# The MoE 1 planner's rate for DMA transposes, 290 to 173 bytes per ns, in a kernel of attention and two MoE layers

## The chip, the cores and the metric

The kernel runs on one core of a Trainium2 chip. The metric is the device time of one execution in microseconds (us); lower is better. Times of before are given as the median of three runs; the profile is one further execution.

## What is computed

Attention over 4 batches, 8 heads, 576 tokens and 64 columns a head, with a mask by blocks of 64; its output, 2304 tokens of 512 columns, goes through MoE 1 (one dense layer with an ELU-like function) and MoE 2 (a skip test, a choice of one of 8 experts for each token, and that expert's two matrices). Cut to the operations:

```python
def _attn_ref(q, k, v):                      # 4 x 8 x 576 x 64
    scores = scale * np.matmul(q, k.transpose(0, 1, 3, 2))
    scores = np.where(block_i >= block_j, scores, -1000000000.0)
    attn = softmax(scores)
    return np.matmul(attn, v)

def _moe_ref(x, w_in, w_out):                # 2304 x 512, 512 x 2048, 2048 x 512
    h = x @ w_in
    g = np.where(h > 0.0, h, np.exp(np.minimum(h, 0.0)) - 1.0)
    return g @ w_out

def _moe2_ref(x, w_skip, w_gate, w1, w2):    # 8 experts, 512 x 1024 and 1024 x 512
    do_compute = x @ w_skip > 0
    e_idx = np.argmax(xc @ w_gate, axis=1)   # xc: the rows of x with do_compute
    h = np.maximum(xc[mask] @ w1[e], 0.0)    # for each expert e
    y[mask] = gate_w[mask, None] * (h @ w2[e])
    out[do_compute] = xc + y
```

## The kernel before

The program has two parts. Its first, which takes some 620 us, holds attention, MoE 1, the routing of all tokens and the preparation of the first experts' weights; a planner puts all of it in one order. Its second runs the experts in blocks of 128 tokens, with a small plan for each block.

*Attention* goes by batch b, head pair p and block row i. `s_unit` computes scores into a PSUM tile s (a ring of 3), `x_unit` takes the row maximum on VectorE (mx) and the exp on ACT (e32), `h_unit` and `l_unit` write the normalised weights as two fp16 halves, high and low, into ehl (ACT writes one, VectorE the other). SP then transposes ehl to et with a DMA transpose, and `pv` multiplies et with v (vt) into the PSUM tile xps (one buffer). k and q are split into halves and transposed by DMA in the same manner (kt, qt).

*MoE 1* takes chunks c of 256 tokens, nine of them. `l1` is the first matrix (PSUM h, a ring of 2), `l1a` and `l1b` the function on ACT and VectorE (g), `l2` the second matrix (PSUM y). The first two chunks run in fp32 on the tiles twi and two, the others in fp16 halves (win, wout). The weights come as 64-bit floats: `raw_load` loads 512 KB of words (rw, 16 times w_in and 16 times w_out), `conv` makes fp32 words of them with three VectorE operations. A load waits for the conversion of the fourth load before it.

*Routing*: `post` scales a tile of y, transposes it by DMA (x2t, 256 KB; the very last tile goes through TensorE), `logits` computes nine columns (lp), `route` and `route2` find expert and place on VectorE, with a small matmul (rp), and store them in lists. When the last chunk is routed, the gathers of the first block (gp, from GpSimd) start, each transposed by DMA (mxt). Two blocks of the first experts (`ahead_block`, matmuls ahp and ya) are gathered a chunk earlier and run meanwhile.

*The order.* Every operation of the first part is recorded as a step with its reads and writes (class `Recorder`), and `order` (line 149) plays the steps through: it keeps for each engine the time at which it is free, for each step the time at which its inputs are there, takes the engine that can go on first, and of its ready steps the one recorded first. What comes out is a fixed order of instructions on each engine; on the chip an engine takes them strictly in that order. `_Engine.cost` (line 310) says how long a step takes. For a DMA on SP there are two numbers: how long SP is busy, and for how long the transfer holds the DMA queue. The second moves `dma_free`, the time until which the queue is taken: SP is not given a new transfer more than 3 us before that time, a transfer ends behind it, and what reads its result may be planned 1.0 us after its end.

```python
if e == "sp":
    f = max(f, dma_free - 3.0)
...
    end = max(t + (1.12 if s[1] < 0.6 else 1.3), dma_free) + s[2]
    dma_free = end
```

Of the kernel before, what the change touches and what calls it, by code (L numbers as in the profile page):

```python
# [267 lines left out]
def _count(ap):  # L268
    n = 1
    for _, c in ap:  # L270
        n *= c
    return n
# [15 lines left out]
class _Engine:  # L288
# [21 lines left out]
    def cost(self, op, k):  # L310
        e = self.e
        out = k["out"]
        if e == "sp":
            b = _count(out.ap) * mybir.dt.size(out.dtype)
            if op == "dma_start_transpose":
                return max(1.2, b / 290e3 + 0.35), b / 290e3
            run = min(a.ap[-1][1] * mybir.dt.size(a.dtype) for a in (out, k["in_"]))
            return 0.48, b / 360e3 * (2 if run < 512 else 1)
        n = _count(out.ap[1:])
        sb = all(x.space == bass.MemoryType.SB for x in (out, k.get("in_", out), k.get("in0", out)))  # L320
        if e == "pe":
            if op == "transpose":
                return 0.2, 0.0
            t = n / 2400.0 * (4 if k["lhsT"].dtype == F32 else 1)
            here = out.offset // out.ap[0][0]
            prev, self.rec.last_pe = self.rec.last_pe, here
            return (0.02 if prev == 0 and here == 64 and n < 400 else max(t, 0.01)), 0.0
        if e == "act":
            aps = any(hasattr(k.get(x), "tensor") for x in ("scale", "bias"))
            return (0.094 if sb else 0.051) + n * 0.833e-3 + 0.093 * (aps + ("accum_out" in k)), 0.0  # L330
        if e == "dve":
            if op == "tensor_reduce":
                n = _count(k["in_"].ap[1:])
            aps = any(hasattr(k.get(x), "tensor") for x in ("scalar", "scalar1", "scalar2"))
            x = 1.0
            if op in ("tensor_copy", "tensor_scalar") and sb:
                x = 0.5 if mybir.dt.size(k.get("in_", k.get("in0")).dtype) == 4 else 0.25
            return 0.069 + n * x / 960.0 + 0.061 * aps, 0.0
        if op == "indirect_dma_start":
            return 1.05, 2.0  # L340
        return 0.15, 0.0
# [1471 lines left out]
```

## Time and profile before

| what | us |
|---|---|
| runs, median of three | 803.34 (802.21 to 807.96) |
| the profiled execution | 801.38 |
| its span, from first to last instruction | 799.7 |
| TensorE busy | 699.3 |
| VectorE busy | 585.4 |
| ScalarE (ACT) busy | 526.9 |
| GpSimd (POOL) busy | 98.3 |

The page of the profile gives for each engine the busy time, for 40 equal slices of the span the busy share and the granted TensorE clock, and groups of instructions with the idle time before them and what ended it. Further answers of the trace give sums by stretches of time, the waits between engines, and the instructions in order of time. PE is TensorE, DVE VectorE, ACT ScalarE, POOL GpSimd, and SP issues the DMAs. Most matmuls of the first part are recorded by one helper and so carry one line, L307; they are told apart by their tiles.

### The profile page before, as it was taken

What the parts mean: (1) busy time and instruction counts of PE and PEld (TensorE: products, weight loads), DVE (VectorE), ACT (ScalarE), POOL (GpSimd) and SP (SyncE); (2) the same over time, 40 slices, a digit from 0 to 9 for tenths busy, and PEclk for the clock granted to TensorE, in tenths of its full rate; (3) what the DMA queues carried; (4) which work ended last, traced back from release to release, by engine and by line L of the source; (5) the groups of instructions that cost most, each with busy time, mean ns of one, the idle gap of its engine ahead of it and who ended that gap; (6) DMA issues with size and microseconds to landing.
All of it is one profiled execution on the core that took longest, in us unless ns stands there. A gap on an engine that the chain in (4) does not pass through costs nothing. (4 is left out here: it accounts for less than half of the span.)

```text
span 799.7 us, 18029 instructions
## 1 busy us (share of the span) xinstructions
PE 699.3 (87%) x6586; PEld 461.1 (58%) x6586; DVE 585.4 (73%) x1721; ACT 526.9 (66%) x1166; POOL 98.3 (12%) x185
## 2 busy tenths in 40 slices
PE   0349868999998998999999999999998848998995
PEld 0238524675465655556646667675766635776763
DVE  3866988887998888987789648997876513737810
ACT  4555655999896886886578537673665425868832
POOL 2000000001001100100100100101040432322112
PEclk9999999999999999999999999999999979999998
DMA  9999999976897799898276089271564699989322
GB/s 226 256 204 291 294 299 256 213 130 122 165 176 139 138 181 202 170 197 155 49 125 143 19 162 374 94 225 40 188 181 141 123 236 236 330 240 216 70 29 39
DMA packets 300437, 141.43 MB, mean 177 GB/s; under 512 B 269659, under 2 KB 277989, under 8 KB 299808
## 3 DMA queue, kind: packets, MB, share of 16 engines
q1 hardware_dynamic: 295568, 130.65, 72.7%
q0 software_dynamic: 4752, 9.33, 4.8%
q8 instruction: 60, 0.98, 0.5%
q14 instruction: 57, 0.47, 0.2%
HBM read 76.20 MB, written 13.41 MB: 112 GB/s over the span
## 5 line engine op out<-in xcount | busy, mean ns | idle before, releaser
L307 PE MATMUL h<-xt,win 128*128 128x256 f16 x1344 | 159.5, 274 | 1.4 <-DVE n L307 1.0
L307 PE MATMUL y<-wout,g 128*128 128x512 f16 x672 | 156.5, 380 | 0.0
L307 PEld LDWEIGHTS <-win 128*128 128x128 f16 x1344 | 128.2, 98 | 28.2 <-issue 5.0
L307 PEld LDWEIGHTS <-g 128*128 128x128 f16 x672 | 62.4, 98 | 70.6 <-issue 5.2
L307 ACT ACTIVATE ehl<-e,su 128x64 f16<-128x64 f32 (+4 forms) x208 | 86.2, 470 | 22.7 <-DVE su L307 9.1
L307 ACT ACTIVATE e<-s,mx 128x64 f32<-128x64 f32 (+7 forms) x160 | 78.5, 492 | 34.0 <-DVE mx L307 16.3
L307 DVE SCALAR_TENSOR_TENSOR ehl<-e,su,ehl 128x64 f16<-128x64 f32 (+4 forms) x208 | 85.9, 442 | 9.8 <-ACT ehl L307 9.4
L307 PE MATMUL s<-kt,qt 128*64 128x512 f16 (+7 forms) x640 | 64.7, 306 | 25.6 <-ACT e L307 14.6
L307 DVE TENSOR_REDUCE mx<-s 128x1 f32<-128x64 f32 (+7 forms) x160 | 70.1, 448 | 11.5 <-PE s L307 11.1
L307 PE MATMUL xps<-et,vt 128*64 128x128 f16 (+1 forms) x1440 | 49.7, 220 | 22.0 <-DMA et<-ehl 19.0
L307 POOL MEMSET ehl<- 128x128 f16 x80 | 16.3, 210 | 403.2 <-DMA et<-ehl 284.2
L307 PEld LDWEIGHTS <-vt 128*64 128x64 f16 x1440 | 41.5, 115 | 39.3 <-issue 23.2
L307 PE MATMUL h<-xt,twi 128*128 128x256 f32 x256 | 63.3, 403 | 0.9 <-DVE g L307 0.9
L307 PE MATMUL y<-two,g 128*128 128x512 f32 x128 | 61.7, 613 | 2.4 <-DVE two L307 2.4
L307 PEld LDWEIGHTS <-qt 128*64 128x64 f16 x640 | 28.8, 115 | 57.8 <-issue 40.8
L307 PEld LDWEIGHTS h<-xt,twi 128*128 128x128 f32 x256 | 50.1, 201 | 10.6 <-DVE g L307 1.3
L307 ACT ACTIVATE el<-h,col 128x512 f32<-128x512 f32 x56 | 38.2, 682 | 25.3 <-PE h L307 25.1
L307 PE MATMUL y<-p,hh 128*128 128x512 f16 x192 | 46.0, 393 | 9.5 <-ACT hh L307 9.1
L307 ACT ACTIVATE g<-el,col 128x512 f16<-128x512 f32 x56 | 40.1, 717 | 19.6 <-DVE el L307 19.4
L307 PEld LDWEIGHTS <-hh 128*128 128x128 f16 x288 | 27.7, 99 | 43.1 <-ACT hh L307 9.6
L1450 DVE SCALAR_TENSOR_TENSOR p<-p,n,p 128x1024 f16<-128x1024 f32 x37 | 47.3, 1282 | 5.1 <-ACT p L1449 5.0
L307 PEld LDWEIGHTS <-p 128*128 128x128 f16 x768 | 45.8, 98 | 8.2 <-issue 3.7
(209 smaller groups left out, 1176.1 us busy)
## 6 DMA issues: line engine op xcount, KB each, us to landing
p<-in_moe_w_dram SPq DMA_DIRECT2D x45, 512.0 KB, 6.6
rw<-in_moe_w_in_dram SPq DMA_DIRECT2D x16, 512.0 KB, 5.1
rw<-in_moe_w_out_dram SPq DMA_DIRECT2D x16, 512.0 KB, 7.4
pb<-in_moe_w_dram SPq DMA_DIRECT2D x14, 512.0 KB, 5.6
vflat<-in_v_dram SPq DMA_DIRECT2D x4, 1152.0 KB, 7.3
out_dram<-pay SPq DMA_DIRECT2D x18, 256.0 KB, 3.5
pay_d<-pay SPq DMA_DIRECT2D x18, 256.0 KB, 2.6
raw<-in_k_dram SPq DMA_DIRECT2D x16, 256.0 KB, 3.9
```

Of the source, the lines that this page charges most:

```text
L307: rec.call(e, time, lambda: getattr(self.real, op)(*args, **kw), reads, writes, dma)
L1450: rc.call("dve", 1.2, lambda: nc.vector.scalar_tensor_tensor(out=half(1), in0=raw.t, scalar=sc, in1=half(0), op0=ALU.mult, op1=ALU.subtrac ...
```

## The change

One number in the planner's cost of a DMA transpose: the time for which it holds the queue in the plan is now its bytes at 173 in place of 290 per ns. The time for which SP is busy with it keeps its 290. No operation, tile or buffer changes.

```diff
--- before.py
+++ after.py
@@ -313,7 +313,7 @@
         if e == "sp":
             b = _count(out.ap) * mybir.dt.size(out.dtype)
             if op == "dma_start_transpose":
-                return max(1.2, b / 290e3 + 0.35), b / 290e3
+                return max(1.2, b / 290e3 + 0.35), b / 173e3
             run = min(a.ap[-1][1] * mybir.dt.size(a.dtype) for a in (out, k["in_"]))
             return 0.48, b / 360e3 * (2 if run < 512 else 1)
```

A transpose of 512 KB, the largest, is planned with 3.0 us of the queue in place of 1.8, one of 128 KB, the smallest, with 0.8 in place of 0.5. All engines' orders change, from near the start up to the first blocks of the experts. Three places:

SP's queue while w_out is loaded (rw, in_moe_w_out_dram; et, qt and kt are transposes, vflat a load of 1.2 MB), before:

```order
L307 DMA rw_142<-in_moe_w_out_dram 128x1024
L307 DMA_TRANSPOSE qt_361<-qq_360 128x16x128
L307 DMA vflat_297<-in_v_dram 128x2304
L307 DMA rw_143<-in_moe_w_out_dram 128x1024
L307 DMA rw_144<-in_moe_w_out_dram 128x1024
L307 DMA rw_145<-in_moe_w_out_dram 128x1024
L307 DMA_TRANSPOSE et_336<-ehl_318 128x12x128
```

and after:

```order
L307 DMA rw_142<-in_moe_w_out_dram 128x1024
L307 DMA rw_143<-in_moe_w_out_dram 128x1024
L307 DMA rw_144<-in_moe_w_out_dram 128x1024
L307 DMA vflat_297<-in_v_dram 128x2304
L307 DMA_TRANSPOSE et_336<-ehl_318 128x12x128
L307 DMA rw_145<-in_moe_w_out_dram 128x1024
```

rw_143 and rw_144 moved ahead of the load vflat_297 and of the transpose qt_361, which has seven more w_out loads ahead of it now.

TensorE in batch 1's second half (xps_745 takes et_719 and then et_728; h_746 and h_773 are groups of MoE 1's first matrix, y_720 of its second, s_749 a score of batch 2; each row stands for a run of like ones with their weight loads), before:

```order
L307 MATMUL xps_745<-et_719,vt_384 64x128
...
L307 MATMUL xps_745<-et_719,vt_485 64x128
...
L307 MATMUL xps_745<-et_719,vt_557 64x128
...
L307 MATMUL h_746<-xt_449,win5_589 128x256
...
L307 MATMUL xps_745<-et_728,vt_384 64x64
```

and after:

```order
L307 MATMUL xps_745<-et_719,vt_557 64x128
...
L307 MATMUL h_746<-xt_449,win5_589 128x256
...
L307 MATMUL y_720<-wout3_631,g_724 128x512
...
L307 MATMUL s_749<-kt_667,qt_670 64x64
...
L307 MATMUL h_773<-xt_449,win6_597 128x256
...
L307 MATMUL xps_745<-et_728,vt_384 64x64
```

Behind et_719 stand now, besides the second half of h_746's matmuls, a group of y_720, the score s_749 and half of h_773 before et_728 is used; twelve of h_746's 24 moved ahead of et_719.

TensorE at the hand-over from MoE 1 to the experts (lp_1443 and lp_1445 are the logits of the last chunk's two tiles, rp_1449 its router matmul, ahp and ya the ahead blocks), before:

```order
L307 MATMUL lp_1443<-wgs_78,x2t_1439 128x9
...
L307 MATMUL lp_1445<-wg32_79,x2t_1442 128x9 x4
...
L1078 MATMUL ya_1494<-p20_7394,hha_1488 128x512
...
L307 MATMUL rp_1449<-oh16_1448,tri16_76 128x8
...
L307 MATMUL rp_1449<-oh16_1448,ones16_75 128x8
```

and after:

```order
L307 MATMUL lp_1445<-wg32_79,x2t_1442 128x9 x4
...
L1078 MATMUL ya_1494<-p20_7429,hha_1488 128x512
...
L307 MATMUL lp_1443<-wgs_78,x2t_1439 128x9
...
L307 MATMUL rp_1449<-oh16_1448,tri16_76 128x8
...
L307 MATMUL rp_1449<-oh16_1448,ones16_75 128x8
```

lp_1443 moved behind lp_1445, behind twelve matmuls of ahp and six of ya.

## Rows read from the trace of the kernel before

**Rows 1.** The page: span, busy time of each engine, granted clock in 40 slices.

```profile
span 799.7 us, 18029 instructions
...
PE 699.3 (87%) x6586; PEld 461.1 (58%) x6586; DVE 585.4 (73%) x1721; ACT 526.9 (66%) x1166; POOL 98.3 (12%) x185
...
PEclk9999999999999999999999999999999979999998
```

**Rows 2.** Sums by stage: stretch, length, busy us of each engine, clock, DMA share, GB/s.

```profile
0.00:55.00 55.00, 13.48 (x151) 9.32 (x151) 35.83 (x110) 29.48 (x81) 4.83 (x41) 1.00 1.08 227
55.00:95.00 40.00, 36.96 (x170) 28.66 (x169) 30.51 (x64) 25.99 (x46) 0.32 (x2) 1.00 1.09 289
95.00:150.00 55.00, 44.78 (x349) 21.47 (x347) 48.48 (x142) 33.55 (x73) 1.53 (x8) 0.99 1.10 261
150.00:480.00 330.00, 316.95 (x3197) 201.34 (x3193) 274.79 (x905) 251.13 (x646) 26.54 (x74) 0.99 0.78 145
480.00:605.00 125.00, 124.02 (x944) 83.83 (x941) 104.13 (x275) 78.36 (x112) 15.34 (x21) 1.00 0.57 188
605.00:629.00 24.00, 18.55 (x276) 14.22 (x274) 13.70 (x77) 10.54 (x27) 4.94 (x5) 1.00 0.45 108
629.00:800.00 171.00, 144.52 (x1525) 102.31 (x1521) 77.99 (x153) 97.82 (x185) 44.82 (x35) 0.95 0.71 169
...
150.00:200.00 50.00, 50.00 (x401) 35.30 (x396) 40.90 (x149) 47.18 (x125) 5.53 (x14) 0.97 0.75 148
```

**Rows 3.** Waits, 95 to 150, and TensorE's of 0 to 150: total us, times, longest.

```profile
PE y L307 <- DVE two L307: 2.4, 4, 1.1
...
DVE two L307 <- DMA rw<-in_moe_w_out_dram: 5.7, 5, 2.4
...
PE s L307 <- ACT e L307: 12.1, 9, 2.9
```

**Rows 4.** Waits of TensorE, 150 to 480.

```profile
PE xps L307 <- DMA et<-ehl: 8.3, 9, 1.8
...
PE xps L307 <- DVE qq L307: 1.1, 1, 1.1
```

**Rows 5.** Sums of two stretches: transposes alone, then copies.

```profile
396.00:413.00 17.00, 16.83 (x149) 8.73 (x148) 12.13 (x40) 11.00 (x32) 1.02 (x5) 1.00 0.54 101
483.00:503.00 20.00, 20.00 (x158) 13.89 (x156) 18.01 (x62) 15.01 (x24) 1.23 (x1) 1.00 1.03 372
```

**Rows 6.** TensorE in order of time: start us, us, what, idle before it.

```profile
253.80 2.79 PE L307 MATMUL h<-xt,win 128*128 128x256 f16 x24
...
258.39 0.66 PE L307 MATMUL xps<-et,vt 128*64 128x64 f16 x30 [1.79 <-DMA et<-ehl]
```

**Rows 7.** The same around 295: twelve y, twelve h and the row behind.

```profile
292.77 2.76 PE L307 MATMUL y<-wout,g 128*128 128x512 f16 x12
295.37 1.47 PE L307 MATMUL h<-xt,win 128*128 128x256 f16 x12
296.68 0.45 PE L307 MATMUL lp<-wgs,x2t 128*128 128x9 f16 x12
```

**Rows 8.** The hand-over on TensorE, VectorE, GpSimd and TensorE again.

```profile
609.20 0.46 PE L307 MATMUL lp<-wgs,x2t 128*128 128x9 f16 x12
609.51 1.04 PE L307 MATMUL lp<-wg,x2t 128*128 128x9 f32 x8
610.40 0.83 PE L1078 MATMUL ahp<-mxt,p 128*128 128x128 f16 x12
611.07 1.46 PE L1078 MATMUL ya<-p,hha 128*128 128x512 f16 x6
...
610.46 0.29 DVE L307 COPY lg<-lp 128x9 f32<-128x9 f32 x2
...
619.94 1.12 POOL L307 DMA_INDIRECT gp<-pay_d,lists  x1 [10.04 <-DVE hha L307]
...
628.62 1.50 PE L307 MATMUL hp<-mxt,p 128*128 128x128 f16 x24 [2.72 <-DMA mxt<-gp]
```

## The prediction

> **What bounds the kernel now.** I read the page's head first [rows 1]: the span is 799.7 us, and TensorE is busy for 699.3 of it (87%), more than any other engine, at a granted clock of 0.9 or more in all slices but one. The change adds and removes no instruction, so those 699.3 us stay. What a new order can move is the rest, some 100 us in which TensorE stands idle, and the next question is where it lies. The sums by stage [rows 2] answer it: length less PE busy gives 41.5 us of idle time in 0 to 55, 3.0 in 55 to 95, 10.2 in 95 to 150, 13.1 in 150 to 480, 1.0 in 480 to 605, 5.5 in 605 to 629 and 26.5 behind that.
>
> These stages have different limits. Up to 150 us the DMA share is above 1: the transfers set the pace, TensorE waits. From 150 to 605 TensorE itself is the limit (441 of 455 us). From 605 to 629 the last tokens are routed and gathered. Behind 629 the instructions of each block stand in the same order before and after, so that I leave its 26.5 us as they are.
>
> Of each stage I then read who waits for whom. From 95 to 150 TensorE lost 2.4 us to VectorE's conversion of the w_out words, and VectorE 5.7 us to the loads of these words [rows 3]. From 150 to 480 it lost 8.3 us in nine waits of an xps matmul for the transpose that fills et [rows 4]; with the smaller rows of that answer this is nearly the whole 13.1.
>
> **Which rate is true.** The planner charges a copy 360 bytes per ns and charged a transpose 290. Two stretches of the queue show each kind alone [rows 5]: from 396 us on SP issues only transposes, from 483 us on almost only 512 KB copies. The transposes move 101 GB/s at a DMA share of 0.54, which is 187 for a full share; the copies 372 at 1.03, which is 361. So 360 was right for copies, 290 too fast for transposes by half, and 173 is 8% on the slow side. The new plan thinks of a transpose's landing about as the chip does; it was too hopeful before, and placed consumers so tightly that nine of them waited.
>
> A rule of the Trainium skill speaks against this: "Advanced Engine Details and Errata", section X-Bar Transpose (TRN2), says that transpose DMAs are as fast as regular ones, at 350 to 400 GB/s. By that rule even 290 was too slow and the change makes the plan worse. The trace does not agree for these shapes, 187 against 361, so this gets a small chance only (last rival).
>
> **The change, term by term.** The sum is made on the profiled execution, 801.4 us (its span and 1.7 us around it). The median of the runs shown is 803.3, which is 2.0 more; I stay on the profiled execution's footing.
>
> 0 to 55: no term. The last transpose before the first MoE 1 matmul (et_263) is the 36th transfer of the queue in both orders, with the same 11.9 MB issued ahead of it, and the DMA share there is 1.08. What goes earlier inside this stretch makes something else later by as much.
>
> 55 to 150, the w_out loads: all of them but the third, and the fourth, which stays where it was, come with fewer bytes ahead of them in SP's queue, mostly by 0.5 to 1.7 MB; the first piece of order above shows two of them jumping ahead of a vflat load of 1.2 MB and a qt transpose of 0.5 MB. At the 261 GB/s of 95 to 150 that is 2 to 6 us earlier. The raw loads and transposes that fall behind them are for batch 1, whose scores come only at the end of this stretch. What a load can give back is the wait for it: 2.4 us on TensorE at least as it stands, 5.7 if VectorE, busy for 48.5 of these 55 us, turns every gap of its own into earlier words; nothing if ACT, whose exps and squares the matmuls of this stretch wait for too, is late by itself. I take the row nearest to the end of the chain, TensorE's: **-2.4** (0 to -5.7).
>
> 150 to 480, the xps matmuls: how long a transpose is covered is the matmul work that stands between the last score of its unit and its first use. The second piece of order shows the longest of the nine waits, 1.79 us at 258.39 [rows 6]. New in front of xps_745<-et_728 are six y matmuls and twelve h ones, some four score matmuls aside. Twelve y matmuls took 2.60 us and the twelve h ones behind them 1.31, by the starts of the following rows [rows 7], so the new work is 1.30 + 1.31 = 2.6 us, more than the wait. I went through the other eight in the same way: for six of the nine the order puts 0.9 to 4 us more in front, for three nothing that counts. Six at the mean of 8.3/9 = 0.92 are 5.5 us saved. The work comes from somewhere: three places have less in front than before, et_998 (2.6 us less), xps_1019 (its one PSUM buffer is now asked for straight behind xps_981, with 0.3 us of work between in place of 5.7), and s_411, with 0.2 us behind the score that frees its buffer in place of 5. At 0.92 each they cost 2.8. Sum: **-2.7** (from -9.4, where all the waits for et with the 1.1 beside them go, to +2.8, where the waits only move and the new ones come on top).
>
> 480 to 605: 1.0 us of idle time is there to win or lose; the pieces only change places by one or two. No term.
>
> 605 to 629, the hand-over: this one is a loss that the order shows. Before, the two logits groups of the last chunk (lp_1443, lp_1445) stood together at 609.20 and 609.51 [rows 8], VectorE copied both at 610.46, and the chain went on through routing, list, gather (619.94) and transpose to the first hp matmul at 628.62, with TensorE idle 2.72 us in front of it. After, the plan expects x2t_1439 later and puts lp_1443 behind lp_1445, twelve ahp and six ya matmuls (third piece of order): from 609.20 on 0.89 for lp_1445 and 0.67 for the ahp ones by the starts of the rows, 1.30 for the ya ones as for six y in rows 7, and its own 0.46, together 3.3 us, so it ends at 612.5 in place of about 609.7, and both logits are there 2.0 us later than 610.5. The router's rp matmul also stands three ya matmuls further back (0.65 us), which the delay hides. Behind the late lp stand only the ahead blocks, which fill TensorE meanwhile but run out before 628. The scatter of the first ahead block now stands in front of the first gathers on POOL; that engine was idle for 10.04 us there and ya ends earlier in the new order, so I cost it at nothing; if its o2 is late, it costs its own issue, some 1.1 us as the gather's row has it. Of the 2.0 us I take **+1.7** (0 if the lists' other inputs came last anyway, +3.1 with the scatter).
>
> Sum: 801.4 - 2.4 - 2.7 + 1.7 = **798.0 us**.
>
> **Rivals.**
> *All the waits go* (the plan is now true, everything lands in time): -5.7 - 9.4 and 0 to +1.7 at the hand-over, with 0.85 taken: 787.1 us. For it speaks that the waits for et are short, 1.8 us at most [rows 4], so that a little more cover cures them; against it that ACT and DVE are behind most of these chains.
> *The waits only move*: -2.4, +1.7 and the et waits as long as before: 800.7 us. For it: TensorE is at 96% from 150 to 480, so whatever is put in front of one consumer is missing in front of another.
> *ACT and VectorE become late* (slower): from 150 to 200 ACT is busy 47.2 of 50 us [rows 2]. The new order moves scores, logits and routing of chunk 0 closer together there, so that more VectorE work stands between a score and its et; where this grows more than the cover, the score buffers stay full and TensorE waits for ACT's exp as it does in the first 150 us, 12.1 us in nine waits [rows 3], 1.34 each. From five such waits on it eats the forecast's gain; eight of them are +10.7, with -2.4 and +1.7: 811.4 us.
> *Transposes are as fast as copies*, so that the plan is now further off: no gain from loads or cover, +2.8 for the new places, +1.7: 805.9 us. The two rates of [rows 5] speak against it. It is what the rule of the Trainium skill named above would bring.
>
> **How the numbers follow.** Forecast 0.42 (its own range 793 to 803), all the waits go 0.26, the waits only move 0.15, ACT and VectorE late 0.12, fast transposes 0.05. One per cent, about what a measurement of this kernel tells from no change, is 8 us: below 793.4 lies the first rival with 0.07 of the forecast's tail, 0.33; above 809.4 the slower rival and 0.03 of tails, 0.15; 0.52 between. The range runs from 784, a little past the fast rival's time, to 810, at the near edge of the slow one's, and leaves out about 0.1 at either end.
>
> **What would show it.** Right: in the changed profile TensorE's waits for VectorE's two shrink below 1 us from 95 to 150, the nine xps waits fall to about six in all with half the time, the second logits group of the last chunk ends near 612 and the first hp matmul behind the gathers has more idle time in front than 2.72 us; PE idle from 150 to 480 is near 10 us. Wrong: that idle time stays at 13 or grows with ACT's exp as releaser (third rival), or falls below 5 (first); or et_263 lands earlier or later than before, which would mean that the start is not held by bytes.

## The result and the profile after

| | before | after |
|---|---|---|
| median of four runs | 802.78 us (800.12 to 807.96) | 812.71 us (809.77 to 814.26) |
| ratio, 95% interval | | 1.0103 [1.0064, 1.0143] |
| profiled execution, its span | 801.38, 799.7 us | 809.77, 808.0 us |

The change cost 1.0%. The forecast of 798.0 had the wrong sign, and its range ended 2.7 us short of the median. The profiled execution is the fastest of the four after, so the trace shows 2.9 us less of the loss than the median. The page's head after, which answers to [rows 1]:

```profile
span 808.0 us, 17999 instructions
...
PE 703.2 (87%) x6586; PEld 465.7 (58%) x6586; DVE 589.1 (73%) x1721; ACT 527.5 (65%) x1166; POOL 97.9 (12%) x185
...
PEclk9999998799999999999999999999999889999998
```

TensorE has the same 6586 matmuls and is busy 3.9 us longer. The clock row has a new dip in the seventh and eighth slice (121 to 162 us). Sums by stage of the kernel after (columns as in [rows 2]):

```profile
95.00:130.00 35.00, 29.81 (x176) 13.47 (x176) 33.27 (x76) 18.49 (x38) 0.61 (x3) 1.00 1.08 307
130.00:160.00 30.00, 21.10 (x202) 12.80 (x202) 24.63 (x100) 23.14 (x54) 1.23 (x6) 0.77 0.96 204
160.00:480.00 320.00, 312.42 (x3157) 198.22 (x3157) 269.66 (x876) 247.73 (x631) 26.18 (x73) 0.99 0.81 145
480.00:520.00 40.00, 36.46 (x270) 23.90 (x269) 32.66 (x83) 26.30 (x40) 1.94 (x2) 1.00 0.60 218
...
605.00:640.00 35.00, 25.27 (x343) 20.15 (x342) 15.92 (x86) 14.24 (x34) 7.55 (x8) 0.92 0.61 130
```

and the same stretches of the kernel before:

```profile
130.00:160.00 30.00, 25.93 (x255) 16.63 (x251) 25.89 (x103) 23.46 (x54) 1.23 (x6) 0.94 1.06 222
160.00:480.00 320.00, 306.95 (x3114) 193.35 (x3113) 266.44 (x872) 242.40 (x624) 26.13 (x72) 0.99 0.77 142
480.00:520.00 40.00, 40.00 (x300) 26.73 (x297) 36.28 (x92) 28.53 (x43) 2.21 (x2) 1.00 0.66 232
...
605.00:640.00 35.00, 28.92 (x390) 21.40 (x387) 21.40 (x91) 17.82 (x40) 9.19 (x9) 1.00 0.51 106
```

So there are two losses of TensorE time ahead of the experts (130 to 160, 480 to 520), one gain (160 to 480) and a loss at the hand-over. Windows at fixed times blur this, since the two programs are not at the same point at the same time. I therefore used a second measure, the **lag**: each program's matmuls are counted in its own order by their columns, laid on its trace, and the time at which a kernel has done as much matmul work as before had done at a given time is compared. It comes from one profiled execution each, and the programs do the work in another order, so a single value is good to some 2 us: five kernels below whose order up to 165 us is that of before stand at +0.6 to +2.2 at 170 (late_173, mid_173, tail_173, mid_handover, mid_pay), so some 1.5 us of a lag there belong to the execution of before itself. Lag of after: about 0 at 130 us (-0.6), **+6.4** at 170, **+0.3** at 480, **+4.0** at 520 and 600, **+7.9** at 660, +8.4 at the end (809.77 less 801.38). By place: start +6.4, middle -6.1, 480 to 520 +3.7, hand-over (600 to 660) +3.9, behind +0.5.

**The start.** SP's queue after, in order of time:

```profile
114.12 0.52 SPq L307 DMA_DIRECT2D rw<-in_moe_w_out_dram  x1
114.69 3.90 SPq L307 DMA_TRANSPOSE qt<-qq  x1
118.68 1.48 SPq L307 DMA_DIRECT2D rw<-in_moe_w_out_dram  x3
...
121.59 0.84 SPq L307 DMA_DIRECT2D raw<-in_k_dram  x1
```

The load of batch 1's next k piece (raw<-in_k_dram) goes out at 121.59, behind the w_out loads. Before, it went at 113.32:

```profile
113.32 0.77 SPq L307 DMA_DIRECT2D raw<-in_k_dram  x1
```

What ACT and TensorE did then, after:

```profile
124.10 0.47 ACT L307 ACTIVATE xt<-xps,col 128x256 f32<-128x256 f32 x1 [1.37 <-PE xps L307]
130.05 0.63 ACT L307 ACTIVATE k<-raw 128x512 f16<-128x512 f32 x1 [5.48 <-DMA raw<-in_k_dram]
...
133.93 1.59 PE L307 MATMUL s<-kt,qt 128*64 128x512 f16 x12 [0.95 <-ACT e L307]
138.67 0.32 PE L307 MATMUL s<-kt,qt 128*64 128x64 f16 x4 [3.15 <-ACT e L307]
...
140.42 3.18 PE L307 MATMUL y<-two,g 128*128 128x512 f32 x4
...
144.82 1.98 PE L307 MATMUL y<-two,g 128*128 128x512 f32 x4
```

ACT works in order: its conversion of that piece waits 5.48 us for the load, the exps (e) stand behind it, the next scores need their PSUM buffer and wait for the exps. TensorE is busy for 5.08 of the 10 us from 130 (7.80 before). Its granted clock is 1.00 from 130 to 136 and 0.53 from 136 to 140, then 0.85 to 150 and 0.66 to 160; the clock has two levels, 1.2 and 2.4 GHz, and these are means over both. Four y matmuls take 3.18 us at 140.42 and 1.98 at 144.82. So the loss has two parts, idle time and then slower work. That this one load is the cause is not shown by these lines; the experiments test it.

**480 to 520.** GpSimd, VectorE and TensorE of after:

```profile
493.01 0.97 POOL L307 DMA_INDIRECT lst_d<-li,si  x1 [24.85 <-DVE li L307]
498.43 0.96 POOL L307 DMA_INDIRECT lst_d<-li,si  x1 [4.45 <-DMA lst_d<-li,si]
...
503.80 0.17 DVE L307 COPY li<-tokid 128x2 f32<-128x2 f32 x1 [4.19 <-DMA lst_d<-li,si]
...
506.56 0.15 DVE L307 CAST cb<-n 128x1 bf16<-128x1 f32 x1
...
506.76 0.16 PE L307 MATMUL ns<-cb,ones 128*128 128x1 bf16 x1 [3.54 <-DVE cb L307]
```

A copy of 0.17 us fills the next chunk's list, li. li has two buffers, and the scatter that reads the older one must have landed. That scatter is now issued at 498.43, among the 512 KB weight loads (DMA share 0.93 from 480 to 500), and VectorE comes to the copy 1.2 us behind it. Before, it went later, and the copy behind it, at 508.31, did not wait:

```profile
504.80 0.98 POOL L307 DMA_INDIRECT lst_d<-li,si  x1 [1.98 <-DMA lst_d<-li,si]
```

After, the copy holds VectorE for 4.19 us; behind it stands the cast cb, and for that a single ns matmul of the weights' norm waits 3.54 us, with all of TensorE's work behind it.

**The hand-over**, which answers to [rows 8]:

```profile
606.95 1.06 ACT L1419 ACTIVATE jk<-pb 128x1024 bf16<-128x1024 f32 x1 [4.54 <-DMA pb<-in_moe_w_dram]
...
608.00 0.67 ACT L307 ACTIVATE pay<-y,col 128x512 f32<-128x512 f32 x1
...
612.13 0.66 PE L307 MATMUL xp<-ident,pay 128*128 128x128 f32 x4 [2.81 <-ACT pay L307]
...
616.80 0.45 PE L307 MATMUL lp<-wgs,x2t 128*128 128x9 f16 x12
...
617.28 0.17 DVE L307 COPY lg<-lp 128x9 f32<-128x9 f32 x1 [0.29 <-PE lp L307]
...
623.74 1.68 POOL L1118 DMA_INDIRECT out_dram<-o,ah  x1 [6.25 <-ACT o L307]
625.73 1.08 POOL L307 DMA_INDIRECT gp<-pay_d,lists  x1 [0.31 <-DVE lists L307]
...
630.13 4.43 SPq L307 DMA_TRANSPOSE mxt<-gp  x2
...
636.64 2.72 PE L307 MATMUL hp<-mxt,p 128*128 128x128 f16 x24 [5.95 <-DMA mxt<-gp]
```

On ACT a square of expert weights (jk<-pb) now stands ahead of pay<-y and waits 4.54 us for its load. Before, pay<-y came first:

```profile
599.45 0.69 ACT L307 ACTIVATE pay<-y,col 128x512 f32<-128x512 f32 x1 [0.68 <-DMA pb<-in_moe_w_dram]
602.36 1.06 ACT L1419 ACTIVATE jk<-pb 128x1024 bf16<-128x1024 f32 x1 [2.23 <-DMA pb<-in_moe_w_dram]
```

Everything that leads to the last chunk's routing follows: logits copied at 617.28 (610.46 before), the first hp matmul at 636.64 behind 5.95 us of idle time (628.62 and 2.72). Those 24 matmuls take 2.72 us in place of 1.50, at a granted clock of 0.50 in place of 1.00. Part comes back: the next wait, of a y matmul for ACT's hh, falls from 9.1 to 5.6 us.

**The middle.** TensorE's waits of after, 170 to 480, which answer to [rows 4]:

```profile
PE s L307 <- ACT e L307: 5.3, 4, 4.0
PE xps L307 <- DVE xt L307: 1.3, 3, 0.6
```

The nine waits for et, 8.3 us, are gone, all of them. (Left out are two rows of 0.3 and 0.2 us.) The one long wait that is left, 4.0 us, has the cause of 480 to 520 once more, on VectorE and then TensorE:

```profile
344.05 0.17 DVE L307 COPY li<-tokid 128x2 f32<-128x2 f32 x1 [4.47 <-DMA lst_d<-li,si]
347.47 0.25 PE L307 MATMUL s<-kt,qt 128*64 128x64 f16 x4 [4.01 <-ACT e L307]
```

The scatter was issued at 338.20; behind the copy stand the steps that ACT's exp and so the score wait for. It is in every kernel that keeps the order of after there (raw_scatter, li_lp, all_four, five_moved, chain_moved: 3.9 to 4.1 us); no experiment moves this copy.

### The profile page after: what moved, and what is told of

It is laid out like the page before. It is cut to its first block, busy times and chain, and to the rows that moved or that the text cites. A ratio compares the mean times of both kernels' runs of the same rounds, so it can differ in the third digit from the quotient of the medians.

```text
span 808.0 us, 17999 instructions
## 1 busy us (share of the span) xinstructions
PE 703.2 (87%) x6586; PEld 465.7 (58%) x6586; DVE 589.1 (73%) x1721; ACT 527.5 (65%) x1166; POOL 97.9 (12%) x185
## 5 line engine op out<-in xcount | busy, mean ns | idle before, releaser
L307 PE MATMUL xps<-et,vt 128*64 128x128 f16 (+1 forms) x1440 | 50.3, 220 | 14.8 <-DMA et<-ehl 10.8
L307 PEld LDWEIGHTS <-p 128*128 128x128 f16 x768 | 48.6, 102 | 11.2 <-issue 6.4
```

Of the source, the lines that this page charges most:

```text
L307: rec.call(e, time, lambda: getattr(self.real, op)(*args, **kw), reads, writes, dma)
```

## The experiments

All times are compared with runs of before on the same chip; lags are against the trace of before.

| kernel | median us | ratio [95%] | lag 170 | 480 | 520 | 600 | 660 | end |
|---|---|---|---|---|---|---|---|---|
| after | 812.71 | 1.0103 [1.0064, 1.0143] | 6.4 | 0.3 | 4.0 | 4.0 | 7.9 | 8.4 |
| late_173 | 803.47 | 0.9994 [0.9964, 1.0024] | 0.6 | -10.9 | -5.0 | -4.7 | -1.6 | 1.6 |
| early_173 | 811.64 | 1.0082 [1.0054, 1.0111] | 5.0 | 5.5 | 5.5 | 5.5 | 6.1 | 6.9 |
| mid_173 | 797.42 | 0.9921 [0.9895, 0.9947] | 1.8 | -9.9 | -9.9 | -8.8 | -6.8 | -6.1 |
| tail_173 | 813.91 | 1.0105 [1.0056, 1.0154] | 2.2 | 1.3 | 7.8 | 7.9 | 12.0 | 14.5 |
| raw_scatter | 813.22 | 1.0132 [1.0091, 1.0174] | 5.9 | -0.1 | 4.0 | 4.1 | 5.4 | 7.5 |
| li_lp | 811.59 | 1.0115 [1.0066, 1.0164] | 7.5 | 1.6 | 1.6 | 1.7 | 8.4 | 9.8 |
| mid_handover | 798.15 | 0.9944 [0.9914, 0.9973] | 1.0 | -10.8 | -10.8 | -9.7 | -4.3 | -1.1 |
| all_four | 810.07 | 1.0086 [1.0058, 1.0115] | 5.6 | -0.6 | -0.6 | -0.6 | 6.7 | 7.2 |
| five_moved | 806.95 | 1.0017 [0.9999, 1.0035] | 5.3 | -0.9 | -0.9 | -0.8 | 0.0 | 3.0 |
| mid_pay | 797.41 | 0.9888 [0.9838, 0.9938] | 2.2 | -9.2 | -9.0 | -6.3 | -6.0 | -3.0 |
| bisect_late | 807.06 | 1.0024 [0.9991, 1.0056] | 5.2 | -1.2 | -1.0 | 1.7 | 3.5 | 4.4 |
| bisect_early | 808.50 | 1.0030 [1.0000, 1.0060] | 6.4 | 2.4 | 2.5 | 3.6 | 3.4 | 6.3 |
| chain_moved | 809.77 | 1.0058 [1.0026, 1.0090] | 8.9 | 3.0 | 3.0 | 3.0 | 4.8 | 8.2 |
| wout_later | 805.63 | 1.0026 [0.9997, 1.0056] | -0.7 | -7.8 | -2.2 | -2.1 | 2.8 | 3.2 |
| wout_tail | 800.81 | 0.9942 [0.9921, 0.9964] | 1.4 | -5.6 | -5.6 | -5.6 | -1.7 | 1.2 |
| wout_173_290 | 800.14 | 0.9941 [0.9920, 0.9962] | -0.9 | -6.7 | -6.7 | -6.7 | -6.3 | -4.6 |

### Which part of the plan does it: four kernels with 173 in a part of it

The cost of a transpose now depends on how many steps the planner has placed; in the plan's own time 950 are placed by about 165 us and 2560 by about 410, ahead of the list and the hand-over.

```diff
-                return max(1.2, b / 290e3 + 0.35), b / 173e3
+                return max(1.2, b / 290e3 + 0.35), -b / 1e3
...
+RATES = ((0, 290), (950, 173))                 # late_173
+RATES = ((0, 173), (950, 290))                 # early_173
+RATES = ((0, 290), (950, 173), (2560, 290))    # mid_173
+RATES = ((0, 290), (2560, 173))                # tail_173
+def _dma(self, i, done):
+    x = self.steps[i][2]
+    return x if x >= 0 else -x / [r for n, r in RATES if n <= done][-1]
```

*late_173*

> The planner uses 290 until 950 steps are placed (about 165 us of the run) and 173 from there; up to 165 us the order is that of before, word for word. Theory A (the places add up: the start costs some 6.5 us, the stretch from 170 to 480 us gives some 6 back by better cover, the end costs some 8): the lag against before is 0 at 170 us, -6 at 480 us, and the whole takes about 803 us. Theory B (the waits for et went because the late start let the transposes get ahead): no gain from 170 to 480, lag 0 at 480 us, the waits for et are back with 5 to 8 us, about 809 us.

*early_173*

> The planner uses 173 until 950 steps are placed (about 165 us) and 290 from there; from about 300 us on the order is that of before. Theory A: lag +6.5 us at 170 us and still +5 to +7 at 480 us and at the end, with the waits for et of 150 to 480 us as long as before (8.3 us): about 808 us. Theory B: the lag shrinks to about 0 by 480 us although the order there is that of before, the waits for et are below 3 us: about 802 us.

*mid_173*

> The planner uses 290 until 950 steps are placed, 173 from there to step 2560 (about 165 to 470 us), 290 again behind that, so that start and end are planned as before. Theory A: lag 0 at 170 us, -6 at 480 us, and it stays there: about 795 us, faster than both kernels. Theory B: lag 0 all along, about 801 us.

*tail_173*

> The planner uses 290 until 2560 steps are placed (about 470 us) and 173 behind that: up to there the order is that of before, from about 500 us on that of the changed kernel. Theory A: lag 0 at 480 us, +3.5 at 520 us (a wait of a norm's sum, ns, for its squares of the late weight loads), about +9 at the first gathered hp matmul, +8 at the end: about 809 us. Rival C (the end costs only because it is reached late, with the rest of the order shifted against the loads): +2 to +3 at the end, about 804 us.

Measured: early alone +0.8%, middle alone -0.8%, tail alone +1.05%; their sum, +1.08%, is the +1.03% of the whole within the intervals. The places add up (theory A); the other theories fall. The trace of tail_173 lost more than foretold, 13 us behind 480 where after lost 8; its median does not show this (the profiled execution, 815.92, is near the slowest of its four). The early part is +5.0 us at 170 and nothing that counts is added behind it. The middle part takes 11 us off between 170 and 480 where the start is left alone. In early_173, whose transposes are planned at 290 from 165 us on, the waits for et are back:

```profile
PE xps L307 <- DMA et<-ehl: 10.7, 11, 1.7
PE s L307 <- DMA qt<-qq: 2.1, 2, 1.1
```

and in mid_173, with 173 there, 0.2 of them are left:

```profile
PE s L307 <- ACT e L307: 1.8, 5, 0.5
...
PE xps L307 <- DMA et<-ehl: 0.2, 1, 0.2
```

So the gain is real. It is the start and the tail that eat it. The 11 us are more than the waits for et (8.3 us); kernels that keep the order of after there gain about 6, and the one long wait at 347 us is part of that difference. mid_173 beats both kernels; no later version beat its median by what can be told.

### Undoing single places of the changed kernel

Steps are taken out of the finished order and put in front of another, with the plan as it was: `raw` the k load ahead of the w_out loads, `li` the copy behind the norm's instructions, `lp` the logits of lp_1443 back ahead of lp_1445, `scatter` that of the ahead block behind three gathers, `et` et_370 ahead of two w_out loads, `pay` the first pay<-y conversion ahead of jk<-pb, and two of the squares that follow (jk<-pd) behind the scaling of pay.

```diff
-        return sorted(done, key=lambda i: (steps[i][6], pos[i]))
+        return self.moved(sorted(done, key=lambda i: (steps[i][6], pos[i])))
...
+MOVES = ((518, 376), (3346, 3408))             # raw_scatter: raw, scatter
+MOVES = ((3021, 3209), (3108, 3110))           # li_lp: li, lp
+MOVES = ((518, 376), (3021, 3209), (3346, 3408), (3108, 3110))  # all_four
...
+    for x, y in MOVES if len(steps) > 2000 else ():
+        order.remove(x)
+        order.insert(order.index(y), x)
```

*raw_scatter*

> The changed kernel's order with two steps put elsewhere: the load of raw_363 (keys of batch 1) ahead of the second load of rw_145, so that four w_out loads, a qt transpose and a v load no longer stand in front of it; and the scatter of the first ahead block on POOL behind the first three gathers. Theory A: ACT's wait of 5.5 us for that load, behind which its exps queue, is what the start costs: it goes, TensorE's waits for ACT's exp at 133 and 138 us (4.1 us) fall below 1, the granted clock from 130 to 160 us is 0.9 or more, and the lag at 170 us falls from 6.4 to 1 or 2 us. The scatter's data stand in front of the gathers' data: without it the first gathered hp waits about 4 us for mxt instead of 5.9. Together about 803 us on the footing of the changed kernel's profiled 809.8. Rival: the start is held by all transfers alike, the wait only goes to another load or transpose, lag at 170 us still 4 or more; the scatter costs only its own issue, 0.2 us: 808 to 810 us.

ACT's wait for the k load went, and nothing came of it. The next wait of the same kind stood right behind (ACT of raw_scatter):

```profile
124.56 0.63 ACT L307 ACTIVATE k<-raw 128x512 f16<-128x512 f32 x1 [0.73 <-PE cn L307]
130.14 1.25 ACT L307 ACTIVATE ehl<-e,su 128x256 f16<-128x256 f32 x3 [4.95 <-DMA et<-ehl]
```

ehl's buffer is read by a transpose, et, that is behind the w_out loads too. The lag at 170 is 5.9 in place of 6.4. The scatter took 1.0 us off the wait for mxt (4.9 for 5.9) and 2.6 off the hand-over's loss, but 2.1 us came back behind 660, and the median is no better: no gain shown.

*li_lp*

> The changed kernel's order with two steps put elsewhere: VectorE's copy li<-tokid (0.17 us of work, it waited 4.2 us at 499.6 us for the scatter of an earlier list) later, behind the third sum of a weight's squares; and lp_1443 of the last chunk in front of lp_1445 again, as before. Theory A: that copy blocked VectorE's queue, and TensorE's ns waited 3.5 us for the cb behind it: the ns wait goes, the lag at 520 us falls from 4.0 to about 0.5; lp_1443 then waits for its transpose and ends 1.0 to 1.5 us earlier, the first gathered hp comes 1 us earlier: together 804 to 806 us on the footing of the changed kernel's 809.8. Rival: ns waits for the squares of the late weight loads on ACT anyway, wait at least 2.5 us: 808 to 809 us.

li was right: the ns wait is gone and 480 to 520 costs nothing (1.6 at 480, 1.6 at 520). lp was wrong. TensorE at the hand-over of li_lp:

```profile
613.65 0.46 PE L307 MATMUL lp<-wgs,x2t 128*128 128x9 f16 x12 [2.61 <-DMA x2t<-pay]
```

x2t is late, as the new plan supposed, so the logits put back in their old place wait for it, and the hand-over costs 6.8 us in place of 3.9. So the move on which my +1.7 rested was no loss of its own.

*mid_handover* (mid_173 with scatter and lp) and *all_four*

> The kernel with 173 from step 950 to 2560 and 290 at either end (797.4 us median, 795.2 profiled), with the scatter behind the first three gathers and lp_1443 in front of lp_1445, as before. Theory A: the wait for mxt in front of the first gathered hp (6.0 us) falls by 2 to 3 us: about 794.5 us median. Rival: the hand-over is held by the routing and the gathers' own landing, no change: 797 us.

> The changed kernel's order with all four steps put elsewhere (raw_363, li, scatter, lp_1443), the rate 173 kept throughout. If the four places carry the whole loss and add up: 809.8 - 5 - 3.5 - 2 - 1 = about 798 us, faster than before and near the kernel that uses 173 only in the middle. If the late transfers behind these steps are the cause and not the steps: 806 to 810 us.

Both carry lp's wait for x2t (2.5 us in mid_handover), and neither gains at the hand-over: 5.4 and 7.3 us lost there. all_four keeps -0.6 from 480 to 600, li's part, and the start's +5.6.

*five_moved* (raw, et, li, pay, scatter) and *mid_pay* (mid_173 with pay, scatter)

```diff
+MOVES = ((518, 376), (536, 384), (3021, 3209), (3083, 3402), (3404, 3096), (3405, 3319), (3346, 3408))  # five_moved
+MOVES = ((3083, 3402), (3404, 3096), (3405, 3319), (3346, 3408))  # mid_pay, with mid_173's RATES
```

> The changed kernel's order with the rate 173 and five places put otherwise: at the start raw_363's load ahead of rw_145 and the transpose of et_370 ahead of the second load of rw_137 (with raw_363 alone ACT then waited 5.0 us for the ehl buffer that this transpose frees); li's copy later; on ACT the first scaling of the last chunk's y (pay) in front of the square of the late weight pb, for which ACT waited 4.5 us, and two squares behind pay's second step; the scatter behind three gathers. lp_1443 stays where the changed kernel has it. Theory A (each loss is an engine's queue that stands behind one late transfer): lag at 170 us 2 to 3 us in place of 6, at 520 us no step, at the first gathered hp 3 us less than the changed kernel's: about 800 us on the footing of its 809.8. Theory D (the start is held by what VectorE and ACT do in which order, and the next wait takes the place of each that goes): lag at 170 us still 5 or more, about 804 us.

> The kernel with 173 from step 950 to 2560 only (797.4 us median), with the same order on ACT for the last chunk (pay in front of the square of pb) and the scatter behind three gathers, lp_1443 not moved. Theory A: the last chunk's logits and so the first gathered hp come 2 to 3 us earlier, 794 to 795 us. Theory D: the gathers and transposes behind it take the gain, 797 us.

five_moved brought the changed kernel back to +0.2%, not told from no change. The wait for mxt is gone in both; the scatter alone took 1.0 us off it (raw_scatter), so the order on ACT is what made it. That order does not need 173 in the tail: mid_173, planned at 290 there, has jk<-pb ahead of pay<-y too, with waits of 4.8 us for its load and 6.0 for mxt. The hand-over costs 0.8 and 0.4 us by 660 (after: 3.9, mid_173: 2.0). But some 3 us come back behind 660 in both, most of it between 720 and 740, where late_173, which moves nothing, loses 2.2 as well; the cause is open. mid_pay's median is mid_173's. The start kept +5.3: with the load and the transpose both moved, ACT waits for VectorE instead (five_moved):

```profile
133.62 0.69 ACT L307 ACTIVATE e<-s,mx 128x512 f32<-128x512 f32 x1 [7.90 <-DVE ehl L307]
```

### What makes the start late

*bisect_late* and *bisect_early*: mid_173 with 173 in the later or the earlier half of the first 950 steps as well (480 are placed by 100 to 110 us).

```diff
+RATES = ((0, 290), (480, 173), (2560, 290))              # bisect_late
+RATES = ((0, 173), (480, 290), (950, 173), (2560, 290))  # bisect_early
```

> 173 from step 480 (about 111 us) to 2560, 290 at either end. If the start's loss comes from the order up to 111 us: lag at 170 us 0 to 2 us, about 797 us as with the switch at 950. If it comes from the order between 111 and 165 us: lag at 170 us 4 to 6, about 802 us.

> 173 up to step 480 (about 111 us), 290 to step 950, 173 to 2560, 290 behind that. If the start's loss comes from the order up to 111 us: lag at 170 us 4 to 6 us, about 802 us. If it comes from the order behind that: 0 to 2 us, about 797 us.

Either half alone brings most of the loss: 5.2 and 6.4 at 170, where kernels with the start of before stand at 0.6 to 2.2. So no single early placement is to blame, and I looked for something that both halves share: how the planner chooses among the loads.

*chain_moved*: five_moved, with nine steps of the k, q and ehl conversions also ahead of VectorE's work on w_out.

```diff
+MOVES = (..., (565, 487), (566, 487), ..., (589, 487), ...)
```

> The kernel with five places moved, and a further step of the start: VectorE's subtractions for k1_385 and ehl_389 (and ACT's steps ahead of them) in front of five conversions of w_out words, behind which ACT's next exp then waited 7.9 us. Theory A (a chain of queues planned around one late load; put right as a whole it gives the loss back): that wait goes, TensorE's waits for ACT's exp at 134 and 138 us (3.1 us) fall below 1, lag at 170 us 1 to 3 in place of 5.3, the whole 799 us on the footing of that kernel's profiled 804.4. Theory D (VectorE is the limit of 95 to 165 us: what goes in front of one consumer is late for another): TensorE's waits move to y for two, lag at 170 us 4 or more, 803 to 805 us.

The wait moves on to the matmuls that need the w_out words (TensorE of chain_moved), and the lag at 170 grows to 8.9:

```profile
124.62 3.50 PE L307 MATMUL y<-two,g 128*128 128x512 f32 x7
131.63 5.50 PE L307 MATMUL y<-two,g 128*128 128x512 f32 x8 [3.51 <-DVE two L307]
```

VectorE is the full engine there (33.27 of 35 us busy in after, 95 to 130): whichever of its two kinds of work goes first, the other is late (theory D). What has to change is how early the w_out words are asked for.

*wout_later*: 173 throughout, but the w_out loads rank 140 steps further back among the candidates, so that batch 1's loads and transposes go first.

```diff
-        rc.sync.dma_start(out=dst, in_=src)
+        rc.base += 140 * (x >= 16); rc.sync.dma_start(out=dst, in_=src); rc.base -= 140 * (x >= 16)
```

> The changed kernel's planner, 173 throughout, with one thing more: the loads of w_out words have a priority 140 steps lower, so that they stand behind the raw loads and transposes of batch 1 in the choice of what SP issues next. If the start's loss is the price of w_out loads that go ahead of batch 1: lag at 170 us 0 to 3 us. If VectorE's and ACT's work as such, or the transposes before 95 us, set it: 4 us or more. What the rest of the order then does (the tail is planned anew) is not foretold: 800 to 812 us.

Sums by stage of wout_later:

```profile
95.00:130.00 35.00, 28.44 (x170) 12.39 (x169) 32.94 (x75) 18.25 (x42) 0.61 (x3) 0.97 1.09 285
130.00:165.00 35.00, 30.88 (x355) 20.51 (x354) 29.46 (x115) 29.84 (x73) 1.63 (x8) 0.98 1.02 200
```

The lag at 170 is -0.7 in place of +6.4, and TensorE is busy 30.88 us of 130 to 165, at a clock of 0.98 (26.10 at 0.80 in after, 30.93 at 0.95 before). The k load goes out at 116.75 (after: 121.59, before: 113.32). So the start's loss comes from the w_out loads' place in SP's choices. The ns wait (3.8) and the one for mxt (5.8) are still there, and the whole is at +0.3%, not told from no change.

*wout_tail* (wout_later with li, pay, scatter) and *wout_173_290* (wout_later with 290 from step 2560 on)

```diff
+MOVES = ((3021, 3209), (3083, 3402), (3404, 3096), (3405, 3319), (3346, 3408))  # wout_tail
+RATES = ((0, 173), (2560, 290))                                                 # wout_173_290
```

> 173 throughout, the w_out loads 140 steps lower in priority, and at the end li's copy later, pay in front of the square of pb, the scatter behind three gathers. If the three causes are the whole loss: no step of the lag at 500 us (it was 3.8 us of wait), 3 us less at the first gathered hp, so 802.9 + 1.7 - 3.8 - 3 = about 798 us on the footing of the profiled run of wout_later, ratio to before about 0.992. If the end's loss comes back elsewhere: 802 to 805 us, ratio 1.00.

> The w_out loads 140 steps lower, 173 up to step 2560 and 290 behind it. Lag against before about 0 at 170 us, -8 at 480 us, and no ns wait behind it, as with the end planned at 290 before: about 797 us, ratio 0.99. If the end costs the same whatever its rate once it is reached 8 us earlier: 803 us.

Both are 0.6% faster than before: with start and tail put right, the rate of 173 pays, by either way of doing the tail. Neither is told from mid_173. In wout_tail the waits for ns and mxt are gone, as foretold, but from 600 to 660 it still loses 3.9 us (wout_later: 4.9); its granted clock is 0.83 from 600 to 610.

## Why the prediction was wrong

- **The true rate** was right. Planned at 173, et is waited for 0 to 1.6 us in all from 170 to 480 (in all kernels with 173 there), at 290 for 8.3, 10.7 and 8.9 (before, early_173, tail_173). By the rule of the Trainium skill in "Advanced Engine Details and Errata", X-Bar Transpose (TRN2), the higher rate would have been the better plan; these runs do not agree with it for this kernel's transposes.
- **"Those 699.3 us stay"**: 703.2. No instruction was added; the clock fell at the new idle stretches (0.77 from 130 to 160; 0.50 at the hp matmuls of 636.64). I had costed idle time as idle time alone. (Two slices of the clock row of before were below 0.9, not one: 0.7 and 0.8.)
- **0 to 55, no term**: no effect by 130 (lag -0.6). The first MoE 1 matmul starts at 58.13 in place of 54.99, behind a longer wait for et (5.1 us in place of 2.9). But executions differ by about as much: it starts at 55.85 to 56.87 in six other kernels with the start of before, at 56.42 to 58.74 in those with the start of after. Whether the landing of et_263 is held by bytes alone stays open.
- **55 to 150, -2.4: here the forecast failed.** What it said of the w_out loads came: they are earlier, and VectorE waits 0.9 us for them in place of 5.7. On TensorE that saved 0.5 us (2.4 to 1.9). The failed step is "The raw loads and transposes that fall behind them are for batch 1, whose scores come only at the end of this stretch". The scores come late (the first at 154.53), but the conversions for them stand in ACT's and VectorE's orders among the exps of batch 0 (k<-raw on ACT at 103.28 and 130.05). I followed SP's order to what the loads feed on TensorE and skipped the in-order engine between. Measured: +6.4 for -2.4, the largest error: 8.8 of the 11.8 us between 798.0 and the profiled 809.8.
- **150 to 480, -2.7**: sign and mechanism right, the size too small: -6.1, and -6 to -12 where the start is not late (-12 with the order of before up to there, -6 to -7 with the w_out loads further back). The sizing went wait by wait from the rows in front of each. Of the three new waits that it took on, those for et_998 and xps_1019 came to 0.2 us; s_411's came, not in this stretch but in the start, and was 3.15 us and not 0.92: s_411 is the score at 138.67. The new wait of 4.0 us at 347.47 was not foreseen. Where the start is planned as before, the bound of -9.4 was the better value.
- **480 to 605, no term**: +3.7. I looked at TensorE's pieces ("the pieces only change places by one or two") and at its idle time, not at what an earlier scatter on GpSimd would meet in the DMA queues and hold up on VectorE. The idle time of before says what there is to win; it does not bound what can be lost.
- **The hand-over, +1.7**: sign right, cause wrong. Second logits late and more idle time in front of hp came as foretold (617.25 for 612.5; 5.95 us), but lp_1443's place is harmless and x2t really late. The longer wait comes from ACT's jk in front of pay<-y: mid_pay, five_moved and wout_tail, which undo that, have no wait for mxt. The term measured +3.9, and the wait grew by 3.2; undone, with the scatter moved too, the loss to 660 is smaller by 1.6, 3.1 and 1.0, and by 2.6 with the scatter alone (raw_scatter), so how much of it the order on ACT makes is not settled.
- **The rivals.** The first came true in the middle and the third in kind, if not in place: scores wait for ACT's exps (8.3 us in 95 to 170, 3.2 before), around 135 us and behind late transfers, where I had put it behind 150 and blamed VectorE. Its 811.4 is nearest to the 812.7, by luck in part: its eight waits were not these. It got 0.12 because I treated a cure of one stage and harm in another as rivals; they came together.

The sum with what was measured: 801.4 + 6.4 - 6.1 + 3.7 + 3.9 + 0.5 = 809.8.

## What to carry to other kernels

A planner's cost that comes nearer to the chip for one kind of transfer also shifts its other choices. Here it cost 1.0% as it stood, and gave 0.8% in the middle alone and 0.6% with one priority and the tail changed too: try it stage by stage, keep it where it pays, and re-tune the priorities elsewhere. When loads change places, follow each one that falls back to the first in-order engine that touches its data, and look at what is queued behind that instruction, on VectorE, ACT and GpSimd as on TensorE. A wait cured by moving one instruction counts as cured only when the end comes earlier: here the k load, the scatter and the order on ACT each took their wait away, and the next one took its place.

## What was not expected of the hardware

- Idle stretches cost more than their length. TensorE's granted clock fell to 0.53 from 136 to 140 us, where it was busy for 0.71 of 4 us; the 24 hp matmuls behind 5.95 us of idle time ran at 0.50 and took 2.72 us, where 1.50 were needed at 1.00, behind 2.72 us of it.
- The small indirect writes of lst_d landed 5.3 us after their issue at 498.43 (DMA share 0.93 from 480 to 500) and 5.8 us after that at 338.20 (0.58 from 338 to 344), and 2.1 us after that at 504.80 of before, where the queues were nearly idle (0.01 from 504.8 to 508). The weight loads alone do not make the difference; what does is open.
